# Two sums of w_out and one scaling moved from VectorE to GpSimd in block 1, and longer runs of warming matmuls in two waits of the opening

## The chip, the cores and the metric

The kernel runs on one core of a Trainium2 chip. The metric is the device time of one execution in microseconds (us), as the median of several runs. The span of a profile, from its first to its last instruction, is some 1.7 to 1.9 us shorter than the time of the same run.

## The reference, cut to what matters

```python
# q, k, v: (8, 8, 576, 64); g_norm: (64,)
kv  = einsum('bhsd,bhse->bhde', k, v)
o   = einsum('bhsd,bhde->bhse', q, kv)
x   = o / sqrt(mean(o*o, -1) + 1e-6) * g_norm            # -> (4608, 512)
ffn = (gelu(x @ w_gate) * (x @ w_val)) @ w_out           # 512 -> 1536 -> 512
out = x + sigmoid(x @ w_res) * ffn
```

The float32 output has 4608 x 512 elements. The kernel works in blocks of 512 tokens; block 1 holds tokens of batch 1, and while it is computed the attention of batch 2 is prepared beside it.

## The kernel before

From block 1 on, the product with w_out is done in seven half-size products instead of eight. That needs sums and differences of the halves of w_out (`wo_t`, made once) and of the hidden values (`hid_sums`, made in each block). The parts that matter:

```python
def a_x(b, j):                         # t *= g_norm, in place, 128x512 float16
    blk, jj = where(b, j)
    nc.vector.tensor_tensor(out=t_t[blk][:, jj, :], in0=t_t[blk][:, jj, :], in1=g16, op=ALU.mult)

def wo_sums(i):                        # 128x1536 float16
    pairs = [(b_of(1, 2), b_of(1, 1)), (b_of(2, 2), wo_t[:, 0]), (b_of(2, 2), b_of(1, 2)), (b_of(2, 1), wo_t[:, 1])]
    sub(nc.vector, wo_t[:, i], *pairs[i])

def s_begin(blk):                      # "the hid sum" below: a difference of two hidden halves, 128x1536
    sub(nc.vector, s_[2], a_of(blk, 1, 1), a_of(blk, 2, 1))

def m_gval(blk, f):                    # one slice of gate and value: PSUM banks gps, vps (four in the pool)
    ...
    nc.scalar.activation(out=ge, in_=gps, func=AF.Gelu)
    nc.vector.tensor_tensor(out=hids[blk][:, f, :], in0=ge, in1=vps, op=ALU.mult)   # frees vps

# the end of a block, others(): products on TensorE, between them VectorE
    prod(w["A"], s_[1], wo_t[:, 1], False)
    sub(nc.vector, w["F"], w["A"], w["d"], ALU.add)      # "wF": the next product into A waits for it
    prod(w["E"], a_of(blk, 1, 2), b_of(2, 1), False)
    pf((0, 0), w["E"])
    prod(w["A"], s_[2], wo_t[:, 2], False)
    ...
    for g in rows:                                       # block 1: the four scalings of batch 1
        g()
    fin((0, 0))                                          # GpSimd: adds the residual
```

Each batch's norm is one chain of twelve operations of 128x40 on VectorE (lines 254 to 262 of the kernel), each dependent on the one before or nearly so. The opening (batch 0) is a list of words, of which `warm3` is three matmuls on zeros.

## Time and profile before

| | before |
|---|---|
| time, median of the runs ahead of the prediction | 346.13 us (345.3 to 347.43) |
| span of the profile | 345.2 us |
| TensorE busy | 331.4 us |
| VectorE busy | 239.3 us |
| GpSimd busy | 96.2 us |
| TensorE starts block 2 (first gate product) | 94.14 us |

The "waits" view names who waited for whom, with sum, number and longest. `orp` is a product of TensorE in batch 2's attention, which waits for VectorE's `kv`; `vps` and `rps` are the value's and the residual's results in PSUM, the banks that TensorE writes to and VectorE or ScalarE reads. A descriptor issue is the GpSimd instruction that starts a DMA (DMA_DIRECT2D). In a timeline a line is start, length, engine, source line, operation and tiles, and in brackets the idle time before. A line that takes longer than its undisturbed twin is called held or blocked here (VectorE's product osb<-th,osb took 1.64 us at 95.94, beside GpSimd's addition, and 0.69 at 130.83, with GpSimd idle). In the table of stretches the columns after the stretch are the busy time of TensorE (PE), its weight loads, VectorE (DVE), ScalarE (ACT) and GpSimd (POOL), then the granted TensorE clock, the DMA share and GB/s. The prediction shows the lines of before.

### The profile page before, as it was taken

To read this page: it belongs to the slowest core of one execution; us is meant where nothing else is said; L and a number is where in the kernel's file an instruction comes from. 1 tells how busy PE (TensorE), PEld (TensorE's weight loads), DVE (VectorE), ACT (ScalarE), POOL (GpSimd) and SP (SyncE) were. 2 spreads that over 40 slices of the span, in tenths; PEclk is the share of its full clock that TensorE was granted. 3 is DMA by queue.
4 is the path that set the end of the run, shared out by engine and by line. 5 is a ranking of instruction groups with operands and counts; after the bars stand their busy time and mean duration, and the time that the engine had idled before them with its cause. 6 is when DMAs were issued, how large, how long until landed. Compare 5 with 4: busy or idle time off the path is not lost.

```text
span 345.2 us, 6148 instructions
## 1 busy us (share of the span) xinstructions
PE 331.4 (96%) x2426; PEld 187.3 (54%) x2426; DVE 239.3 (69%) x448; ACT 150.2 (43%) x265; POOL 96.2 (28%) x115
## 2 busy tenths in 40 slices
PE   8699999999879999999999999999999999999992
PEld 3454454445734485448544764476447644764481
DVE  6655459789896987698578976885688735443643
ACT  3663474364326352535263615361736133623350
POOL 2783242530082018200820083005000600050013
PEclk9999999999999999999999999999999999999998
DMA  8999999696639473956394539744003120030004
GB/s 237 309 182 204 195 203 174 176 162 53 140 137 171 36 123 120 176 50 133 128 171 37 106 115 168 80 96 156 11 0 61 63 76 2 2 123 0 0 2 122
DMA packets 76399, 38.81 MB, mean 112 GB/s; under 512 B 42066, under 2 KB 73810, under 8 KB 76370
## 3 DMA queue, kind: packets, MB, share of 16 engines
q0 software_dynamic: 38752, 17.17, 40.0%
q1 hardware_dynamic: 37184, 20.71, 22.1%
q10 hardware_dynamic: 434, 0.52, 0.5%
q8 instruction: 19, 0.31, 0.4%
q14 instruction: 10, 0.08, 0.1%
HBM read 38.80 MB, written 9.44 MB: 140 GB/s over the span
## 4 chain that ended last, share of the span: by engine, by line
PE 71%; DVE 1%; POOL 0%; POOLq 0%; issue 0%; DVEq 0%
PE gps L336 21%; PE vps L336 21%; PE wA L427 10%; PE rps L356 7%; PE wF L427 3%; PE w L427 2%; PE wE L427 2%; PE wD L427 2%; PE kvp L187 1%; PE op L205 1%; DVE hid L325 0%; POOL osb L515 0%; PE orp L233 0%; POOLq L998 0%; DVE osb L511 0%
## 5 line engine op out<-in xcount | busy, mean ns | idle before, releaser
L324 ACT ACTIVATE ge<-gps 128x512 f16<-128x512 f32 x108 | 64.3, 597 | 133.1 <-PE gps L336 126.7
L325 DVE TENSOR_TENSOR hid<-ge,vps 128x512 f16<-128x512 f16 x108 | 73.7, 684 | 60.6 <-PE vps L336 58.5
L336 PE MATMUL gps<-xT,wg 128*128 128x512 f16 x424 | 109.0, 379 | 0.0
L336 PE MATMUL vps<-xT,wv 128*128 128x512 f16 x424 | 108.8, 379 | 0.0
L466 POOL TENSOR_TENSOR osb<-osb,t 128x512 f32<-128x512 f32 x28 | 36.7, 1328 | 178.6 <-DVE osb L462 156.6
L336 PEld LDWEIGHTS <-wv 128*128 128x128 f16 x424 | 41.5, 98 | 50.0
L336 PEld LDWEIGHTS <-wg 128*128 128x128 f16 x424 | 40.2, 98 | 45.3 <-issue 0.2
L427 PEld LDWEIGHTS <-hid_s 128*128 128x128 f16 x384 | 37.5, 98 | 6.0 <-issue 1.4
L356 PE MATMUL rps<-wr,xT 128*128 128x512 f16 x144 | 32.7, 379 | 0.0
L427 PEld LDWEIGHTS <-hid 128*128 128x128 f16 x288 | 28.2, 98 | 5.0
L365 ACT ACTIVATE th<-rps 128x512 f32<-128x512 f32 x36 | 21.5, 598 | 18.4 <-PE rps L356 18.4
L356 PEld LDWEIGHTS <-xT 128*128 128x128 f16 x144 | 14.1, 98 | 16.8
L224 DVE TENSOR_REDUCE ss<-sq 128x8 f32<-128x512 f32 x32 | 20.6, 679 | 2.9 <-ACT sq L222 2.7
L427 PE MATMUL wA<-wo_ts,hid_s 128*128 128x256 f16 x168 | 20.6, 273 | 1.2 <-DVE wF L404 1.2
L370 ACT ACTIVATE th<-th 128x512 f32<-128x512 f32 x36 | 19.9, 622 | 0.0
L282 DVE TENSOR_TENSOR t<-op,ny 128x512 f16<-128x512 f32 x28 | 17.8, 681 | 0.1
L296 DVE TENSOR_TENSOR t<-t,g 128x512 f16<-128x512 f16 x36 | 17.4, 536 | 0.1
L222 ACT ACTIVATE sq<-op 128x512 f32<-128x512 f32 x28 | 15.3, 596 | 4.5 <-PE op L205 4.1
L404 DVE TENSOR_TENSOR hid_s<-hid 128x1536 f16<-128x1536 f16 x16 | 15.3, 954 | 0.3
L515 POOL TENSOR_TENSOR osb<-osb,t 128x512 f32<-128x512 f32 (+1 forms) x4 | 4.3, 1078 | 27.8 <-DVE osb L511 27.8
L373 PE MATMUL fps<-wo,hid 128*128 128x512 f16 x48 | 11.2, 379 | 0.0
L427 PE MATMUL wF<-wo,hid_s 128*128 128x256 f16 x84 | 10.3, 273 | 0.0
(133 smaller groups left out, 319.2 us busy)
## 6 DMA issues: line engine op xcount, KB each, us to landing
out_dram<-osb SPq DMA_DIRECT2D x14, 512.0 KB, 2.6
qraw<-in_q_dram POOLq DMA_DIRECT2D x7, 512.0 KB, 8.1
kraw<-in_k_dram POOLq DMA_DIRECT2D x7, 512.0 KB, 9.8
v<-in_v_dram POOLq DMA_DIRECT2D x7, 512.0 KB, 11.6
out_dram<-osb SPq DMA_DIRECT2D x5, 256.0 KB, 3.1
wg<-in_moe_w_gate_dram POOLq DMA_DIRECT2D x2, 512.0 KB, 9.2
wv<-in_moe_w_val_dram POOLq DMA_DIRECT2D x2, 512.0 KB, 9.8
wo<-in_moe_w_out_dram POOLq DMA_DIRECT2D x2, 512.0 KB, 13.6
```

The source lines that it names most:

```text
L222: nc.scalar.activation(out=sq, in_=src, func=AF.Square)
L224: nc.vector.tensor_reduce(out=out_, in_=sq, op=ALU.add, axis=mybir.AxisListType.X)
L282: nc.vector.tensor_tensor(out=t, in0=o, in1=scale, op=ALU.mult)
L296: nc.vector.tensor_tensor(out=t_t[blk][:, jj, :], in0=t_t[blk][:, jj, :], in1=g16, op=ALU.mult)
L324: nc.scalar.activation(out=ge, in_=gps, func=AF.Gelu)
L325: nc.vector.tensor_tensor(out=hids[blk][:, f, :], in0=ge, in1=vps, op=ALU.mult)
L336: nc.tensor.matmul(ps[:, j0 * P : j1 * P], lhsT=w[:, cc, :], rhs=xT_t[blk][:, j0:j1, cc, :], start=(cc == 0 and j0 == 0), stop=(cc == NP - ...
L356: nc.tensor.matmul(rps, lhsT=xT_t[blk][:, j, cc, :], rhs=wr16[:, cc, :], start=(cc == 0), stop=(cc == NP - 1),)
L365: nc.scalar.activation(out=th, in_=rps, func=AF.Tanh, scale=0.5)
L370: nc.scalar.activation(out=th, in_=th, func=AF.Copy, scale=0.5, bias=0.5)
L427: nc.tensor.matmul(ps[:, e - es[0], :], lhsT=a[:, f, e * P : (e + 1) * P], rhs=b[:, f, :], start=(start and e == es[0] and f == 0), stop=( ...
L466: nc.gpsimd.tensor_tensor(out=res_all[of], in0=res_all[of], in1=t_t[blk][of], op=ALU.add)
```

## The change

VectorE is full around the end of block 1 (busy for 9.80 of the 9.90 us from 80.3 on), and TensorE waits for it twice: there (1.2 us at wA) and early in block 2 (1.8 us at orp). The change takes two of the sums of w_out and the four scalings of batch 1 from VectorE to GpSimd; the sums are cut into three pieces each. Six more warming matmuls go into two waits of the opening, against the dip of TensorE's clock there (0.50 from 15.55 to 18.96 us in the trace of before).

```diff
-    def a_x(b, j):
+    def a_x(b, j, eng=nc.vector):
...
     def wo_sums(i):
-        sub(nc.vector, wo_t[:, i], *pairs[i])
+        if i in (0, 2):
+            sub(nc.vector, wo_t[:, i], *pairs[i])
+            return
+        for f in range(0, NFH, 2):
+            sub(nc.gpsimd, wo_t[:, i, f : f + 2, :], *(x[:, f : f + 2, :] for x in pairs[i]))
...
-            for g in rows:
-                g()
...
-    ... o0 warm2 vc2P ... t1 warm1 sq2 ...
+    ... o0 warm3 warm2 vc2P ... t1 warm3 warm1 sq2 ...
...
-        return plan, [lambda j=j: a_x(b, j) for j in range(NJ)]
+        return plan, [lambda j=j: a_x(b, j, nc.gpsimd) for j in range(NJ)]
...
-                plan.setdefault(4, []).append(lambda: wo_sums(1))
-                plan.setdefault(5, []).append(lambda: wo_sums(3))
+                plan.setdefault(6, []).append(lambda: (wo_sums(1), wo_sums(3)))
+                plan.setdefault(9, []).extend(rows)
```

More of the change, by code (lines that the diff above doesn't have):

```diff
@@ L292, in a_xT @@
         )
-    def a_x(b, j):
+    def a_x(b, j, eng=nc.vector):
         blk, jj = where(b, j)
-        nc.vector.tensor_tensor(out=t_t[blk][:, jj, :], in0=t_t[blk][:, jj, :], in1=g16, op=ALU.mult)
+        eng.tensor_tensor(out=t_t[blk][:, jj, :], in0=t_t[blk][:, jj, :], in1=g16, op=ALU.mult)
     def d_qT(b):
@@ L434, in prod, with out_by_products @@
                 )
-    def out_by_products(blk, rows=()):
+    def out_by_products(blk):
         w = {}
@@ L830 @@
     qc1P qc0A qT1 qT0 kc1P kc0A qo0D warm3 lv0D lk0P qo1A warm3 vc1D vc0A kv1 qc2A kv0 kvo1 kvo0 o1 kc2P qT2
-    lk1P lv1D sq1 qo2D o0 warm2 vc2P sq0 rd1 kv2 qc3P rt1 kvo2 rd0 kc3A qT3 wg1 wv1 ri1 o2 rt0 t1 warm1 sq2 vc3D
+    lk1P lv1D sq1 qo2D o0 warm3 warm2 vc2P sq0 rd1 kv2 qc3P rt1 kvo2 rd0 kc3A qT3 wg1 wv1 ri1 o2 rt0 t1 warm3 warm1 sq2 vc3D
     rd2 qo3A xT1 kv3 wg2 wcg0P rt2 kvo3 ri0 ri2 warm2 o3 t2 xo1A wcg1P sq3a wcv0P sq3b g1 xT2 rd3a wcv1P rd3b
@@ L945, in products @@
                 s_rest(blk)
-                outs.extend(out_by_products(blk, late_rows if blk == 1 else ()) if blk < B else out_last(blk))
+                outs.extend(out_by_products(blk) if blk < B else out_last(blk))
             plan.setdefault(NF - 1, []).append(products)
@@ L971 @@
             late = [[g] for g in stores] + [[] for _ in range(NJ)]
-            late_rows = rows
 _INS = ['q', 'k', 'v', 'g_norm', 'moe_w_gate', 'moe_w_val', 'moe_w_out', 'moe_w_res']
```

## The prediction

> **What bounds the kernel now.** I read the page first, then the table of stretches, the waits, the timelines of block 1 (tokens 512 to 1023, computed at 57.5 to 94.1 us) and the opening.
>
> ```profile
> PE 331.4 (96%) x2426; PEld 187.3 (54%) x2426; DVE 239.3 (69%) x448; ACT 150.2 (43%) x265; POOL 96.2 (28%) x115
> ...
> PE 71%; DVE 1%; POOL 0%; POOLq 0%; issue 0%; DVEq 0%
> ```
>
> TensorE is the bound: busy 331.4 of 345.2 us, and nearly alone on the chain that ended last. Only 13.8 us are idle, about 7 of them at the end, which the change doesn't touch. So nothing here can bring 2% (6.9 us); what can move is the few waits of TensorE that the change aims at. The waits view names two behind block 1:
>
> ```profile
> PE orp L233 <- DVE kv L194: 1.8, 1, 1.8
> ...
> PE wA L427 <- DVE wF L404: 1.2, 1, 1.2
> ```
>
> In both TensorE waits for VectorE. The table of stretches (PE, PEld, DVE, ACT, POOL busy) shows why:
>
> ```profile
> 72.50:80.30 7.80, 7.80 (x38) 3.53 (x36) 7.26 (x21) 4.52 (x8) 0.00 (x0) 1.00 1.56 178
> 80.30:90.20 9.90, 8.69 (x64) 6.15 (x63) 9.80 (x18) 5.63 (x10) 0.00 (x0) 1.00 0.13 18
> ```
>
> VectorE has 9.80 of 9.90 us full before the first wait, and GpSimd nothing at all. That is what the change wants to use. VectorE's timeline there:
>
> ```profile
> 75.88 0.95 DVE L404 TENSOR_TENSOR hid_s<-hid 128x1536 f16<-128x1536 f16 x1
> ...
> 77.94 0.18 DVE L254 TENSOR_SCALAR nm<-ss 128x40 f32<-128x40 f32 x1
> ...
> 80.36 0.68 DVE L325 TENSOR_TENSOR hid<-ge,vps 128x512 f16<-128x512 f16 x1
> ...
> 69.61 0.95 DVE L404 TENSOR_TENSOR wo_ts<-wo,wo_ts 128x1536 f16<-128x1536 f16 x1
> 71.09 0.69 DVE L325 TENSOR_TENSOR hid<-ge,vps 128x512 f16<-128x512 f16 x1 [0.53 <-PE vps L336]
> ```
>
> The two sums that leave VectorE end at 70.56, and after them VectorE still waits 0.53 us for TensorE. They cost nothing where they are. From 73.5 on VectorE has no gap, and the twelve tiny operations of the norm run from 77.94 to 80.36 in the middle of it.
>
> Opening, in stretches of 2 us:
>
> ```profile
> 12.00:14.00 2.00, 0.94 (x14) 0.76 (x14) 1.87 (x5) 0.64 (x2) 1.86 (x4) 1.00 1.08 380
> 14.00:16.00 2.00, 1.17 (x14) 0.78 (x12) 1.97 (x5) 1.43 (x4) 2.00 (x4) 0.89 1.02 326
> 16.00:18.00 2.00, 2.00 (x12) 1.16 (x10) 1.27 (x5) 1.20 (x4) 2.00 (x4) 0.50 1.37 188
> 18.00:20.00 2.00, 1.73 (x13) 0.97 (x12) 1.47 (x4) 1.21 (x4) 2.00 (x4) 0.76 1.22 160
> ```
>
> TensorE is half idle from 12 to 16 us, and from about 15.55 to 18.96 its clock is 0.50. The warming matmuls are meant for that.
>
> [...]
>
> ```profile
> 93.63 2.38 DVE L296 TENSOR_TENSOR t<-t,g 128x512 f16<-128x512 f16 x4
> 95.94 1.64 DVE L462 TENSOR_TENSOR osb<-th,osb 128x512 f32<-128x512 f32 x1
> ...
> 94.47 2.55 POOL L466 TENSOR_TENSOR osb<-osb,t 128x512 f32<-128x512 f32 x2 [22.01 <-DVE t L296]
> ```
>
> Four scalings take 1.42 us with GpSimd idle (at 86.92) and 2.38 beside the additions at 94.47; the product at 95.94 takes 1.64 us, where an undisturbed one takes 0.69. Products with one input in PSUM are not stretched. [...] GpSimd's additions of 128x512 at 57.84 (four in 4.95 us, the last stretched by a copy) start 1.11 to 1.13 us apart[...]. [...] The trace's dip lasts 3.41 us and follows a stretch of equal length with some 43% of matmul work[...].
>
> **The change part by part.**
>
> Warming. A warming matmul takes 0.216 us. The first place gets three more before a wait of 1.28 us: they end at 12.13, before the next work at 12.93. The second gets three more before 15.24, ending at 14.9. Neither lies on the path at full clock. In the stretch 12.14 to 15.55 the work rises from 1.48 to 2.13 us (43 to 62%)[...]. If the dip goes, at most 3.41 / 2 = 1.7 us, but the path then hangs on VectorE: the last kv product ends 0.5 us earlier, while VectorE is busy until 16.03 instead of waiting until 16.40 (0.37), and the matmuls after it save 0.22. That is 0.6 us. With even odds: minus 0.3.
>
> The two sums on GpSimd. Removed from VectorE: 2 x 0.95, worth 0 (above). Added: six pieces of 128x512 at 1.11 us. Nothing holds them, so they start when the last descriptor issue of
>
> ```profile
> 71.06 1.40 POOL L79 DMA_DIRECT2D qr<-in_q_dram  x2
> ```
>
> ends, at 72.46, wherever they stand in the program. The scalings, four more at 1.11, follow at once: their data has been there since 56.6. Ten operations, 11.1 us, so at least until 83.6.
>
> What they meet. The hid sum at 75.88 goes first or waits up to 1.1; it holds GpSimd up by 0.8. Piece 5 then starts at about 77.7 and the norm at 77.9. The norm's operations have their inputs in SBUF, so each waits for the GpSimd operation under way[...]. Six GpSimd operations (pieces 5 and 6, four scalings) each block one tiny operation for 0.8 to 1.05 us: 5.7 us in all. The norm ends at about 86.1 instead of 80.4, and GpSimd is then through.
>
> On the path. The residual's second product (81.0) needs the PSUM bank that the hid product at 80.36 reads: no slack. TensorE stops for about 5.7 us there; the 1.2 us wait for wF stays, as VectorE is late by the same 5.7. So block 1 is longer by 5.7.
>
> What comes back. Four scalings leave VectorE behind block 1: 4 x 0.335 = 1.3 us, and the blocked parts there (1.0 on the fourth, 1.0 on the product). VectorE then reaches kv before TensorE needs it, so the wait of 1.8 us at orp and two neighbouring gaps of 0.2 each go: minus 2.2. A gap of 5.7 us may also halve the clock once; most of that hides behind VectorE, so I add 0.4 (an estimate: 1.7 us less the 1.2 us wait, rounded down).
>
> Sum: 5.7 - 2.2 + 0.4 - 0.3 = +3.6 us, so 349.7.
>
> **The rivals.** First: the tiny operations are not blocked (40 elements may slip in, or float16 on GpSimd is fast, with the ten operations done by 79 us). Then the delay is one or two waits, 1.2 us, against 2.2 returned: with 0.3 of the opening, minus 1.3, or 344.8. For it: no tiny operation meets GpSimd in the trace of before (all take 0.19 to 0.20), so the blocking is unproved for that size; and cutting the sums in pieces suggests that someone counted on the lock. Against: larger operations with the same inputs are all blocked. Second: the opening decides, the clock dip goes in every run, 0.6 to 1.7 us, and block 1 is neutral: 345. The runs of before spread over 2.1 us[...]. Third: GpSimd in float16 is slower[...], plus a clock dip on the path: 5.7 + 2.5 + 1.3 - 2.2, about 353.4.
>
> **Range and chances.** I give the main course 0.7 (348 to 352), the faster rivals together 0.25 (344.5 to 346), the slow one 0.05. The weighted middle is 349.0; 344.6 to 352.5 should hold it 8 times in 10. Faster by 2% needs 339.2, out of reach of all waits together: 0.01. Slower by 2% needs 353.1: 0.07. The rest, 0.92, is within 2%.
>
> **What would show it.** Right: GpSimd busy from 72.5 to about 84 in ten operations of 1.1 us; rows of the norm in block 1 of about 1 us instead of 0.2; a wait of TensorE of 5 to 6 us at the residual's products; no wait at orp; the clock at 1.00 from 14 to 20 us or a dip elsewhere. Wrong: norm rows of 0.2 us beside a busy GpSimd (then the first rival holds), GpSimd rows far from 1.1, or sums that start later than 73, past the norm.

The sum: 5.7 - 2.2 + 0.4 - 0.3 = +3.6 us, so 349.7. The 5.7 is the estimate from the trace of before: GpSimd's additions there start 1.11 to 1.13 us apart, and beside them VectorE's four scalings took 2.38 us for 1.42 and a product 1.64 for 0.69, about 0.95 more each. That the tiny operations would each be held by that much, one after the other, no trace had shown. In the same trace the copies of q and k took 1.66 and 1.04 us beside the additions, undisturbed 0.69 and 0.68; hid products, with one input in PSUM, took 0.67 to 0.69 beside them (at 59.52 and 61.71), and 0.69 at 64.70 without. The 0.4 is worked out from the dip of before (3.41 us at 0.50); that a gap brings such a dip was the guess then. The third rival's 2.5 and 1.3 are guesses too.

## The result, and the profile after

The changed kernel takes 350.42 us (350.05 to 350.8, four runs) against 345.84 us for the kernel before in the same rounds. The ratio is 1.0125, 95% interval 1.0088 to 1.0161. A ratio here is the mean time of one kernel's fast runs over that of the other's of the same rounds, so not quite the ratio of the medians. Executions over 1.5% slower than the fastest of the same kernel are left out of the means. It is 1.3% slower, inside the 2% that counts as the same, and clear of noise.

First VectorE's timeline of block 1 after the change, then GpSimd's of the same time:

```profile
73.90 0.68 DVE L325 TENSOR_TENSOR hid<-ge,vps 128x512 f16<-128x512 f16 x1
74.50 7.42 DVE L404 TENSOR_TENSOR hid_s<-hid 128x1536 f16<-128x1536 f16 x1
81.84 0.67 DVE L224 TENSOR_REDUCE ss<-sq 128x8 f32<-128x512 f32 x1
82.43 0.67 DVE L325 TENSOR_TENSOR hid<-ge,vps 128x512 f16<-128x512 f16 x1
83.03 0.17 DVE L254 TENSOR_SCALAR nm<-ss 128x40 f32<-128x40 f32 x1
```

```profile
71.03 6.75 POOL L404 TENSOR_TENSOR wo_ts<-wo,wo_ts 128x512 f16<-128x512 f16 x6
77.71 5.21 POOL L296 TENSOR_TENSOR t<-t,g 128x512 f16<-128x512 f16 x4
```

The ten GpSimd operations run one behind the other from 71.03 to 82.92 ("the run" of GpSimd, below). The hid sum, which took 0.95 us before, takes 7.42 here: it is blocked for 6.47 us, across five boundaries between GpSimd operations, and gets in only ahead of the tenth, which takes 1.89 us instead of 1.16 to 1.18. The tiny operations of the norm meet no GpSimd operation that computes; they take 0.17 to 0.20.

TensorE in the same time, and the stretches with its clock:

```profile
83.16 1.86 PE L336 MATMUL vps<-xT,wv 128*128 128x512 f16 x4 [5.12 <-DVE hid L325]
84.82 5.45 PE L356 MATMUL rps<-wr,xT 128*128 128x512 f16 x16
90.10 1.47 PE L431 MATMUL wA<-wo,hid 128*128 128x256 f16 x12
```

```profile
80.00:82.00 2.00, 0.00 (x0) 0.00 (x0) 2.00 (x2) 0.00 (x0) 2.00 (x2) 0.92 0.01 1
82.00:84.00 2.00, 0.84 (x3) 0.29 (x3) 1.90 (x8) 0.00 (x0) 0.92 (x1) 0.50 0.00 0
84.00:86.00 2.00, 2.00 (x6) 0.73 (x5) 1.79 (x8) 0.00 (x0) 0.00 (x0) 0.50 0.00 0
```

The last value product needs the PSUM bank that the hid product at 82.43 reads, and waits 5.12 us. The clock falls to 0.50 in this wait, for 6.83 us (81.68 to 88.51). The residual's 16 matmuls take 5.45 us instead of 3.62.

The balance, from the starts of the same work in the two profiles:

| TensorE starts | before | after | difference |
|---|---|---|---|
| third slice of block 0 | 22.85 | 21.46 | -1.39 |
| block 2, first gate product | 94.14 | 99.27 | +5.13 |
| the batch's output products in block 2 | 104.32 | 107.48 | +3.16 |
| end of the span | 345.2 | 348.4 | +3.2 |

Block 1 costs 6.5 us, 2.0 come back behind it (the wait at orp is gone from the list of waits), and from there on nothing differs. The 1.39 us of the opening belong to one profile of before that had its clock dip there; the experiments show whether they are the change's. Counted from the third slice to block 2, free of the opening, block 1 takes 71.29 us before and 77.81 after; the experiments use this stretch too.

### The profile page after: what moved, and what is told of

It is laid out like the page before. It is cut to its first block, busy times and chain, and to the rows that moved or that the text cites. A ratio compares the mean times of both kernels' runs of the same rounds, so it can differ in the third digit from the quotient of the medians.

```text
span 348.4 us, 6165 instructions
## 1 busy us (share of the span) xinstructions
PE 333.9 (96%) x2432; PEld 188.1 (54%) x2432; DVE 240.5 (69%) x442; ACT 150.1 (43%) x265; POOL 108.3 (31%) x125
## 4 chain that ended last, share of the span: by engine, by line
PE 89%; DVE 3%; DMA 3%; issue 2%; POOL 1%; POOLq 0%; SPq 0%; DVEq 0%
PE vps L336 26%; PE gps L336 26%; PE wA L431 11%; PE rps L356 9%; PE fps L373 3%; PE wE L431 3%; PE wD L431 3%; PE wF L431 3%; PE w L431 2%; DMA hid_s<-in_v_dram 2%; PE kvp L187 2%; DMA kf<-in_k_dram 1%; PE op L205 1%; DVE t L748 1%; DVE hid L325 1%
## 5 line engine op out<-in xcount | busy, mean ns | idle before, releaser
L356 PE MATMUL rps<-wr,xT 128*128 128x512 f16 x144 | 34.5, 394 | 0.0
L404 DVE TENSOR_TENSOR hid_s<-hid 128x1536 f16<-128x1536 f16 x16 | 21.7, 1358 | 0.3
L296 DVE TENSOR_TENSOR t<-t,g 128x512 f16<-128x512 f16 x32 | 15.0, 520 | 0.1
L659 PE MATMUL idle<-zeros 128*128 128x512 f16 x25 | 9.4, 518 | 1.2 <-DVE zeros L632 1.2
```

What stands on the lines that cost most here:

```text
L356: nc.tensor.matmul(rps, lhsT=xT_t[blk][:, j, cc, :], rhs=wr16[:, cc, :], start=(cc == 0), stop=(cc == NP - 1),)
L404: eng.tensor_tensor(out=out_, in0=in0, in1=in1, op=op)
```

## The experiments

### Warming alone

```diff
 # the kernel before, with
-    ... o0 warm2 vc2P ... t1 warm1 sq2 ...
+    ... o0 warm3 warm2 vc2P ... t1 warm3 warm1 sq2 ...
```

> The kernel before with only the six added warming matmuls. Theory: in the changed kernel's profile the clock stayed at 1.00 through the opening and the third gate product (the first with four matmuls on one line) began at 21.46 us instead of 22.85, so this alone should win 1.4 us: about 344.4, with no clock of 0.50 before 24 us. Rival: [...]the median stays within 0.5 us of 345.8 and some runs keep the dip.

345.94 us against 346.29; ratio 0.9998 (0.9969 to 1.0027). The table of stretches of its profile:

```profile
14.00:16.00 2.00, 1.83 (x18) 0.95 (x16) 2.00 (x6) 1.50 (x5) 2.00 (x4) 1.00 1.19 327
16.00:18.00 2.00, 1.27 (x11) 0.58 (x10) 1.97 (x5) 1.65 (x5) 2.00 (x4) 1.00 1.45 195
...
102.00:104.00 2.00, 2.00 (x7) 0.61 (x5) 0.00 (x0) 0.60 (x1) 2.00 (x4) 0.50 1.02 112
```

The rival was that the opening without a dip was chance. There is no dip in the opening, and the third slice starts at 21.40 as in the changed kernel; but in this run the clock dips behind the wait at orp instead (101.1 to 104.5), and the end is where before had it. The theory's 1.4 us are not there. The next run settles why.

### The move to GpSimd alone

```diff
 # the changed kernel, with the opening of before
```

> The changed kernel without the added warming matmuls. Theory: block 1 costs 6.5 us up to the start of block 2 and gives 2.0 back, so plus 4.6 against before, about 350.4 to 351.8 (the opening's gain of 1.4 missing in the wait-free part). The hid sum is blocked for about 6.5 us behind ten GpSimd operations. Rival (the loss comes from elsewhere[...]): under 348.

350.73 us against 346.29; ratio 1.0138 (1.0107 to 1.0169). Its opening has no added warming, yet no dip either: the clock is 1.00 from 12 to 20 us and the third slice starts at 21.51. So this opening has the dip in some executions and not in others: the profiles of e3, e4 and e10 have the opening of before and no dip there either, that of e11 has one. The whole loss is the move's. The hid sum takes 7.38 us, as in the changed kernel:

```profile
74.54 7.38 DVE L404 TENSOR_TENSOR hid_s<-hid 128x1536 f16<-128x1536 f16 x1
```

### The sums alone

```diff
 # the kernel before, with
+        for f in range(0, NFH, 2):
+            sub(nc.gpsimd, ...)                       # wo_sums(1) and (3), issued at slot 6
```

> The kernel before with only the two w_out sums on GpSimd in six pieces; the scalings stay on VectorE. Theory of one lock held through the whole unbroken run: GpSimd runs from 72.5 to 79.2, the hid sum due at 75.9 is blocked until about 78.5 to 79 (2.6 to 3.1 us), TensorE stops some 2.5 us at the residual's products, nothing is returned, so 348 to 349.5. Rival, turn by turn at every boundary (my prediction's model): the hid sum waits at most 1.1 us, the tiny norm operations some more, 347 to 348.

348.16 us; ratio 1.0061 (1.0027 to 1.0095). On VectorE:

```profile
74.12 3.03 DVE L404 TENSOR_TENSOR hid_s<-hid 128x1536 f16<-128x1536 f16 x1
```

The hid sum is blocked for 2.08 us (3.03 - 0.95) and gets in ahead of the sixth piece; it was kept out at one boundary on the way. The wait at orp stays 1.8 us: nothing is returned. Taking two sums off VectorE costs time, as both theories said. The one lock expected 2.6 to 3.1 us of blocking and the rival at most 1.1, and the measured 2.08 fits neither figure. It is what the changed kernel showed: VectorE is kept out until the last operation of the run and gets in ahead of that one, while the one-lock figure had counted to the run's end.

### The scalings alone

```diff
 # the kernel before, with
-            for g in rows: g()                        # VectorE, inside others()
+                plan.setdefault(9, []).extend(rows)   # a_x(b, j, nc.gpsimd)
```

> The kernel before with only batch 1's four scalings on GpSimd, issued behind the loads. GpSimd runs from 72.5 to 77.0; under the theory of one lock for the run the hid sum due at 75.9 waits 1.1 us, which reaches TensorE as about 1.1; 2.0 come back behind block 1. So about 345 (minus 0.9). Rival, that the return needs the sums to have left too: 347.

344.73 us; ratio 0.9964 (0.9936 to 0.9991), as expected. The hid sum takes 1.89 us, blocked for 0.94 by the last scaling; the wait at orp is gone. The helpful half of the change is the scalings.

### The pieces in turn

```diff
 # the changed kernel, with
+        for f in range(0, NFH, 2):
+            for i in (1, 3):                          # piece of sum 1, then the piece of sum 3 that reads it
+                sub(nc.gpsimd, wo_t[:, i, f : f + 2, :], ...)
```

> The changed kernel with the same ten GpSimd operations, but the pieces of the two sums taken in turn, so that the 2nd, 4th and 6th depend on the one just before and must wait for its end. Theory A ([...]any real wait between two operations lets VectorE in): the hid sum, due at about 74.5, gets in when the 3rd piece ends or the 5th, waits at most 2 us instead of 6.5. Then the tiny norm operations meet the rest of the run, which has no waits: the first of them is blocked until the run ends near 83. Theory B (VectorE gets in at every boundary once it waits, the 6.5 us having another reason): no difference from the changed kernel. Total under A between 347 and 350.5.

348.99 us; ratio 1.007 (1.002 to 1.012). VectorE:

```profile
74.35 0.95 DVE L404 TENSOR_TENSOR hid_s<-hid 128x1536 f16<-128x1536 f16 x1
75.22 0.68 DVE L224 TENSOR_REDUCE ss<-sq 128x8 f32<-128x512 f32 x1
75.81 0.68 DVE L325 TENSOR_TENSOR hid<-ge,vps 128x512 f16<-128x512 f16 x1
76.41 1.06 DVE L254 TENSOR_SCALAR nm<-ss 128x40 f32<-128x40 f32 x1
```

The hid sum gets in at once, at a boundary where GpSimd had to wait for its own result. Theory B, which expected no difference, is out. Theory A was that GpSimd operations which follow one another without a wait keep VectorE out together. It missed the second half: it expected the first tiny operation to be blocked until the run's end. Instead six of the first eight tiny operations take 1.03 to 1.15 us, one per GpSimd operation, as the prediction had it. The norm ends at 84.18 (85.52 in the changed kernel), and TensorE waits 4.3 us at the residual. From the third slice to block 2 it takes 76.57 us, 1.24 less than the changed kernel; the ratios' intervals overlap.

### A start from idle

```diff
 # the changed kernel, with, ahead of the ten,
+    nc.gpsimd.tensor_copy(out=hold, in_=hids[1][0:1, 7, 0:1])     # waits for VectorE
```

> The changed kernel with one tiny GpSimd copy ahead of the ten, that waits for the hid product at about 72.8, so that the run starts from an idle GpSimd instead of from the tail of descriptor issues. In the changed kernel's trace operations of the run overlapped by 0.10 us at first and 0.06 at the end, and VectorE got in only where the overlap had shrunk to 0.05; the additions of before, which start from idle, overlap by 0.03 and let VectorE in at each boundary. Theory C (the overlap[...] is what shuts VectorE out): the overlap is 0.03, the hid sum gets in after one operation (at most 1.1 us), and the tiny norm operations are then blocked one by one, 4 to 5 times by about 1 us. Theory A (unbroken run, whatever its start): the hid sum is blocked until the run ends near 84, so about 352.

350.47 us (three runs 350.16 to 350.62 and one of 354.03, unexplained); ratio 1.0129 (1.0075 to 1.0183). GpSimd, then VectorE, then TensorE:

```profile
73.06 0.18 POOL L942 COPY hold<-hid 1x1 f16<-1x1 f16 x1 [1.84 <-DVE hid L325]
73.21 7.46 POOL L404 TENSOR_TENSOR wo_ts<-wo,wo_ts 128x512 f16<-128x512 f16 x6
```

```profile
74.63 1.66 DVE L404 TENSOR_TENSOR hid_s<-hid 128x1536 f16<-128x1536 f16 x1
...
77.40 1.05 DVE L254 TENSOR_SCALAR nm<-ss 128x40 f32<-128x40 f32 x1
78.49 1.07 DVE L255 TENSOR_SCALAR ny<-nm 128x40 int32<-128x40 int32 x1
```

```profile
86.74 3.17 PE L356 MATMUL rps<-wr,xT 128*128 128x512 f16 x8 [5.97 <-DVE hid L325]
```

Neighbouring GpSimd records overlap by 0.03 to 0.04 us here, and VectorE gets in at every boundary at which it waits: the hid sum is held for 0.7 us, and seven tiny operations for 0.9 us each. Theory C's picture came about, theory A's did not. TensorE waits 5.97 us at the residual's second product, as the prediction had it for the changed kernel. Still the total is that of the changed kernel. The run begins 2.2 us later and ends at 85.09, and the norm ends at 86.09.

The order in which the two engines take their turns decides only a part of the loss, then. VectorE's chain (hid sum, norm, hid product) meets GpSimd at many points here, and eight operations of it are held, for 0.7 to 0.9 us each; or, in the changed kernel, one is held until the last operation of the run, for 6.47 us. Either way it is through about 1 to 2.6 us after GpSimd (86.09 against 85.09 here, 85.52 against 82.92 in the changed kernel). Here the later start of the run takes back what the order gains; in e5, with the run starting as in the changed kernel, the norm ends 1.34 us earlier.

### The sums whole

```diff
 # the changed kernel, with
-        for f in range(0, NFH, 2):
-            sub(nc.gpsimd, wo_t[:, i, f : f + 2, :], ...)
+        sub(nc.gpsimd, wo_t[:, i], *pairs[i])         # 128x1536
```

> The changed kernel with each sum as one GpSimd operation of 128x1536 instead of three pieces. [...]cutting gains nothing: two operations of about 3.3 us, the hid sum blocked as long as before (6 to 7 us), 350.4 within 0.7. If the cut helps, this is slower by 1 us or more; if longer operations mean fewer overlaps and VectorE gets in between the second sum and the first scaling, the hid sum waits about 4 us and it is faster by about 1.

349.05 us; ratio 1.0064 (1.0016 to 1.0113): its third expectation, an entry between the second sum and the first scaling, though after a wait of 2.7 us and not 4. Three runs gave 349.01 to 349.06; a fourth gave 354.29, counts as slow and is not in the ratio. On VectorE:

```profile
74.42 3.69 DVE L404 TENSOR_TENSOR hid_s<-hid 128x1536 f16<-128x1536 f16 x1
```

Its first expectation was that cutting gains nothing. The hid sum takes 3.69 us, and three tiny operations then take 1.05 to 1.19. Cutting the sums gained nothing. It is not slower than the changed kernel, and by the two runs' ratios it may be faster, though the intervals overlap.

### The gap filled

```diff
 # the changed kernel, with, in m_gval for the last slice of block 1
+            for _ in range(20):
+                nc.tensor.matmul(gps, lhsT=zeros[:, 0:P], rhs=zeros, start=True, stop=True)
```

> The changed kernel with 20 warming matmuls ahead of the last gate product of block 1 (into its own bank, which the product then overwrites), so that TensorE works through most of its 5.1 us wait and the clock should stay at 1.00 there. Theory: block 1's lateness is VectorE's alone; the half clock of 81.7 to 88.5 us cost TensorE 2.6 us of its own time, but all of it in the shade of VectorE, since wF came 6.5 us late anyway. Then no change: within 0.5 us of 350.4, with a wait at wF back. Rival: the dip costs its 2.6 us (or the 1.4 that is left after the 1.2 of the wF wait); then 347.8 to 349.

350.1 us (349.77 to 350.37); ratio 1.009 (1.007 to 1.0109) against runs of before that were slower on this chip (347.08). TensorE:

```profile
76.64 4.48 PE L350 MATMUL gps<-zeros 128*128 128x512 f16 x20
80.96 1.03 PE L336 MATMUL gps<-xT,wg 128*128 128x512 f16 x4
82.85 1.02 PE L336 MATMUL vps<-xT,wv 128*128 128x512 f16 x4 [0.86 <-DVE hid L325]
...
94.98 1.47 PE L434 MATMUL wA<-wo_ts,hid_s 128*128 128x256 f16 x12 [1.06 <-DVE wF L407]
```

The clock stays at 1.00 through block 1. The hid sum takes 7.48 us here, and VectorE's wF starts 20.11 us after the hid sum was due (74.12 to 94.23); in the changed kernel it was 20.05 (74.50 to 94.55). From the third slice to block 2 it takes 77.82 us, in the changed kernel 77.81. So the dip had no visible cost: VectorE set the pace, and what TensorE saves it waits for at the residual (1.13 us) and at wF (1.06). The ratios of the two kernels' separate rounds differ by more than that, but their intervals overlap and the runs of before differ between chips.

### The scalings early, with and without warming

```diff
 # the kernel before, with the scalings ahead of batch 3's loads
+                plan.setdefault(4, []).append(
+                    lambda: nc.gpsimd.tensor_copy(out=hold, in_=b16_t[2, "k"][0:1, 0, 0, 0:1])
+                )
+                plan.setdefault(4, []).extend(rows)   # a_x(b, j, nc.gpsimd); no longer in others()
```

> Proposal: the kernel before with the warming of the change and only the scalings on GpSimd, but ahead of the loads, after a tiny copy that waits for the copy of k to be done (63.4), so that the four run from about 63.5 to 68, where VectorE has no operation with two SBUF inputs but the first sum at 67.5. The loads start about 1.7 us later. Expected: the opening's 1.4 and the 2.0 behind block 1, both: about 342.4. If the later loads of batch 3 reach VectorE's copies at 88 us late, part of the 2.0 is lost, 343 to 344.

343.6 us (five runs 343.38 to 343.7 and one of 347.66, unexplained); ratio 0.9926 (0.988 to 0.9972). The 342.4 expected had counted on the opening's 1.4 us, which e1 did not show. Without the warming:

> The proposal of scalings early, without the six warming matmuls. Theory, after the run with warming alone showed no gain: the warming has no part in the proposal's time either, so the same as with it, 343.6 within 0.7. Rival: the warming's 1.4 us show only when nothing later dips the clock; then 345.

343.38 us (343.27 to 343.88); ratio 0.9897 (0.9877 to 0.9917) on another chip. So the warming has no visible part in it. This version beats both kernels, by about 1% against before. Its GpSimd line, the one line of VectorE that it holds, and all that is left of TensorE's waits for VectorE in block 1:

```profile
61.95 4.48 POOL L296 TENSOR_TENSOR t<-t,g 128x512 f16<-128x512 f16 x4
```

```profile
65.87 1.38 DVE L404 TENSOR_TENSOR wo_ts<-wo,wo_ts 128x1536 f16<-128x1536 f16 x1
```

```profile
PE wA L427 <- DVE wF L404: 1.2, 1, 1.2
```

The four scalings run from 61.95 to 66.43, where VectorE reads PSUM up to 65.87 (such products took 0.67 to 0.69 us beside GpSimd's additions in the trace of before, 0.67 beside its sums in e6); then the first of the two sums meets the last scaling and takes 1.38 us instead of 0.95. The loads behind them start 0.9 us later than before (67.85 for 66.96). Neither costs time: from the third slice to block 2 it takes 71.30 us, before 71.29. The wait at orp is gone, and no dip stands in its profile ahead of the tail.

### All ten early

```diff
 # the changed kernel without added warming, with
-                plan.setdefault(6, []).append(lambda: (wo_sums(1), wo_sums(3)))
-                plan.setdefault(9, []).extend(rows)
+                # at slot 4: the same tiny copy of k, then rows, then the six pieces
```

> All ten GpSimd operations of the change (four scalings, six pieces), without the added warming, ahead of the loads from about 62 to 73 us, where VectorE has only products with one input in PSUM. The loads start some 11 us later than before, 7 later than with scalings alone. Theory: the two sums gave nothing where they were, so moving them frees nothing: as the scalings alone early, 343.6 within 0.7, if the loads still come in time; if batch 3's q and k come late, VectorE's copies hold wF up and it is 344 to 347. Rival: 1.9 us less on VectorE in block 1 is worth up to 1.2 (the wait at wF): 342.4.

344.09 us; ratio 0.9917 (0.99 to 0.9934): the theory's 343.6 within 0.7, not the rival's 342.4. The ten run from 62.86 to 74.03, the hid sum takes 0.95 us at 75.19, and wF still comes late, with a TensorE wait of 1.5 us. Taking the sums off VectorE frees nothing, even where they block nothing. Two tiny operations take 0.42 and 0.35 us here instead of 0.18, while descriptor issues of the loads, which start 7.5 us later than before, run beside them.

## Why the prediction was right or wrong

**The size and the direction** were right: 350.42 in a range of 344.6 to 352.5, with the main course at 349.7 and the weighted middle at 349.0. That the size came so near is partly luck. Another operation was blocked than the one foreseen, and the two terms that were not found (plus 0.4, minus 0.3) nearly cancel. It is not all luck: the length of GpSimd's run was foreseen, and VectorE's chain is through 1 to 2.6 us after that run in both pictures.

**The two sums, worth 0 on VectorE:** right. The sums alone made the kernel slower, and all ten early are no faster than the scalings early. The second rival, that the opening decides, is out with e1 and e2.

**Ten operations of 1.11 us from 72.5 to 84:** right (71.03 to 82.92, with an opening 1.4 us earlier). In float16 an undisturbed operation took 1.14 us (the scaling at 80.63 in e6), in float32 1.15 (the additions of before); the third rival, a slower float16, is out.

**What they meet:** this is the step that failed. "The hid sum at 75.88 goes first or waits up to 1.1" was wrong: it was blocked for 6.47 us. I took it from the additions of before that VectorE gets in at each boundary (the copy of q, due at 60.12, took 1.66 us there for 0.69, less than one addition more); for a run that starts behind descriptor issues it did not. "Six GpSimd operations ... each block one tiny operation" then didn't happen in the changed kernel, and its sign, norm rows of about 1 us, failed (0.17 to 0.20). It does happen where VectorE gets in: e5, e6 and e7 show tiny operations of 1.03 to 1.19 us. The first rival, that 40 elements slip in, is therefore out, though the changed kernel's own profile seemed to speak for it.

**On the path, 5.7:** mis-sized by 0.8. The measured term is the 6.47 us of the hid sum, which pass through VectorE's chain whole: wF starts 13.59 us after the hid sum is due before, 20.05 after. TensorE's stop is at the last value product, one product earlier than I said, and the wait at wF of 1.2 us did not stay; the dip took its place, and it is back in e9.

**What comes back, minus 2.2:** right; measured 5.13 - 3.16 = 1.97.

**The dip, plus 0.4:** no cost was found. TensorE loses time to it, but under VectorE's chain (e9).

**The warming, minus 0.3:** no gain was found. Its interval, in microseconds of 346.29, is -1.1 to +0.9. My 0.6 with even odds came from a profile with a dip in the opening, which comes in some executions only. The stretch ahead of it (12.14 to 15.55) holds 1.65 us of work by the table of stretches, 48%, not 1.48 (two more small misreadings carry no weight: block 1 holds rows 576 to 1087, and the tiny operations take 0.18 to 0.20 us before). Of six profiles with the opening of before, one has a dip there at 15.55, one (e11) at 14.80, and e2, e3, e4 and e10 have none. None of the seven profiles with the added warming has one there. So the warming may prevent this dip, or it is chance; in e1 the dip came later, at 101.08, and nothing was won.

With the measured terms the sum is 6.47 - 1.97 = 4.5 us, against 350.42 - 345.84 = 4.6.

Open: why GpSimd keeps VectorE out at some boundaries. What goes with it in part is the overlap of neighbouring GpSimd records (their ends are rough): VectorE was kept out at 0.059 to 0.086 us in the changed kernel and let in at 0.053, and at 0.031 to 0.037 in e5 and e6. But in e3 it was kept out at 0.069 and let in at 0.070, and in e9 kept out at 0.038, so the overlap is no rule. Another regularity holds in all four profiles in which the run starts right behind the descriptor issues, none of its operations waits, and the hid sum meets more than its last one: the hid sum got in ahead of the last operation of the run and no earlier (the tenth of ten in the changed kernel, e2 and e9, the sixth of six in e3). After a wait between two GpSimd operations (e5, e7) or an idle start (e6) VectorE got in at each boundary at which it waited. What makes the difference is not shown.

## What to carry to other kernels

Before moving work to GpSimd, list what VectorE does in the same microseconds with its inputs in SBUF: a product of 128x512 took 1.64 us beside GpSimd for 0.69, the copy of q 1.66 for 0.69 (both in the kernel before), the hid sum 7.42 for 0.95 in the changed kernel. The list goes down to the smallest: in the chain of 128x40 operations, 0.17 to 0.20 us each, those that were held took 1.03 to 1.19 (e5 to e7), about as long as a GpSimd operation. Not all operations on SBUF were held: the reduction of 128x512 took 0.67 beside GpSimd's sums in e6, and 0.68 before, with GpSimd idle. Cutting GpSimd's work into pieces gained nothing here (350.42 us in pieces, 349.05 whole); put the whole run where VectorE reads PSUM (here 62 to 66 us, for 343.38 us), and hold it there with a dependency rather than by its place in the program. Work that VectorE does ahead of a point where it is already waiting was free here (the two sums, 0.95 us each, ahead of a wait of 0.53), and moving it gained nothing (e3, e11).
